# A linear attention and FFN kernel on one core: zero matmuls spread at the start, the last quarter stored in two parts, a new order of all steps

## The chip, the cores and the metric
The kernel runs on 1 core of one Trainium2 chip. The metric is device time in microseconds (us); the median of several executions is compared.

## The reference
Linear ("cosformer") attention on q, k, v of 8 batches x 8 heads x 576 positions x 64, followed by a feed-forward network (FFN) on the 4608 x 512 rows that it gives.

```python
r = np.maximum(x, 0.0)                            # phi, of q and of k
q_p, k_p = concat([r * c, r * s], axis=-1)        # c, s: cos and sin of pi/2 * pos / S
kv  = np.einsum('bhsf,bhsd->bhfd', k_p, v)
z   = np.sum(k_p, axis=2)
num = np.einsum('bhsf,bhfd->bhsd', q_p, kv)
den = np.einsum('bhsf,bhf->bhs', q_p, z)[..., None] + 1e-06
x   = (num / den).transpose(0, 2, 1, 3).reshape(4608, 512)
h   = x @ w_in                                    # w_in: 512 x 2048
out = np.maximum(0.01 * h, h) @ w_out             # w_out: 2048 x 512, out: 4608 x 512 float32
```

## The kernel before
The rows are worked in nine groups g: the first 512 positions of each of the 8 batches (g = 0 to 7), and the 8 x 64 rows left over (g = 8). Groups 0 and 1 take a plain first matrix product (`f0.*`, `f1.*`), and group 0 a plain second one (`F0.*`). All others use a form with seven products for eight blocks (Strassen-Winograd): DVE forms sums of blocks (X of x, S of the activations g, W and T of the weights), PE does the products, and DVE or ACT combine them.

Nothing schedules the kernel but one string, `ORDER` (L31 to L136). Each token is a step, `name[:engine][@slot]`; the program walks through the tokens in turn and emits the instructions of each step, so the order in the string is the order on every engine's queue. `:A`, `:D` and `:P` put a step on ACT, DVE or POOL, and `@` names the slot of a buffer or of a PSUM bank that its tile takes. What a step waits for follows from the tiles that it reads and overwrites. The steps that matter here:

- `i.n`: one matmul of zeros (L295), 128x128 by 128x512, into a PSUM slot of its own. 14 run in one slot before all else, and 16 more stand in the order between real work.
- `Lq`, `Lk`, `Lv`, `Lw1`, `Lw2`, `lq`, `lk`, `lv`: loads, all issued by SP. `cw`, `w`: casts of weights to f16. `v0.c`: cast of a quarter of v. `rq`, `rk`: relu of q or k. `kt`: k times the angles (DVE).
- `qt0.jp.hg`, `qo0.jp.hg`: the q turn of batch 0 on PE, a quarter each, and its copy to `qpT`. `kv0`, `ko0`: the kv sums and their copy. `n`, `N`: numerators on PE, and the division (DVE, three instructions: `den`, `rden`, `xs`). `xt`, `xo`: transpose of x and its copy; `xT`: the same by a DMA transpose, from group 2 on.
- `f`, then `e` (plain) or `b s u y z a c e d` (seven products): the first FFN product and what takes it out of PSUM. `F g.n.tt.h`: product n of the second one, half `tt` of the rows, half `h` of the depth, four matmuls each.
- `S g.n`: sums of activations. Product 1 starts a chain X in PSUM; `M g.1` copies it out (`mid`), and product 2 (`F g.2`) then adds on top of the same bank. `O g.n` adds a chain and a kept part to a quarter of the result in `osb`, and `D g.n` stores that quarter.

For g = 8 a quarter's rows belong to two halves of the partitions, so a store is a pair: SP stores one half, ACT the other. The quarters n = 3 and n = 5 are taken out and stored in two parts (`result_apart`, `store_apart`), n = 2 and n = 4 whole.

Of the kernel before, what the change touches and what calls it, by code (L numbers as in the profile page):

```python
# [11 lines left out]
ALU = mybir.AluOpType  # L12

P = 128
# [33 lines left out]
lq2@3 kv1.1@1 F0.2.14 ko1.1:A F0.0.14 n1.0.1@0 O0.2:D@3 N1.0.1 F0.3.12 F0.3.14 rq2.1:A F0.1.6 F0.1.8
rq2.0:P lk2@2 xt1.1.0@1 xt1.0.0@0 q2.3.0:P q2.0.1:P q2.2.0:P O0.3:D@0 q2.1.1:D lv2.0@1 n1.1.1 N1.1.1
O0.0:A@1 xt1.0.1@0 F0.1.10 xo1.0.1:D q2.3.1:A xo1.0.0:A xo1.1.0:A F0.1.12 f1.2.0@0 f1.0.0@1  # L50
xt1.1.1@0 lk3@0 lv2.1 f1.4.0 q2.0.0:D q2.1.0:P rk2.1:P rk2.0:A xo1.1.1:A f1.1.0 F0.1.14 kt2.0.0
kt2.1.0 kt2.0.1 T1 f1.3.0 f1.4.2 f1.2.2 f1.1.2 f1.0.2 f1.3.2 v2.1:P q2.2.1:D v2.0:A O0.1:A@2 e1.0
e1.1 kt2.1.1 T3 T2 T4 f1.5.0 qT2.0 lq3@3 f1.5.2 e1.2 f1.10@1 rk3.0:A f1.11 kv2 kt3.0.0 f1.6@0 e1.5
kt3.0.1 ko2:A rk3.1:A f1.7 e1.3 rq3.1:A n2.0 f1.12@1 N2.0 f1.13 e1.6 rq3.0:P q3.1.0:A q3.0.0:P n2.1
qT2.1 lv3.0@1 q3.2.0:A lv3.1 kt3.1.0 N2.1 q3.0.1:P f1.8@0 q3.3.0:P q3.1.1:P f1.9 S1.1a n2.2
F1.2.0.0@1 f1.14@1 f1.15 lq4@2 N2.2 n2.3 F1.1.0.0@0 F1.1.1.0 F1.2.1.0 q3.3.1:D e1.4 S1.1b S1.2a e1.7
F1.1.0.1 F1.1.1.1 F1.2.1.1 F1.2.0.1 v3.1:P v3.0:A M1.1:A F1.6.0.0@0 F1.6.1.0 N2.3 S1.1c S1.2b S1.3c
S1.2c F1.6.0.1 F1.6.1.1 kt3.1.1 S1.3a W0.3:D M1.6 W1.3:D S1.3b S1.4a kv3 xT2 F1.7.1.0 F1.7.0.0
F1.7.0.1 X2.1:D X2.2:D ko3:A q3.2.1:A f2.0.1 b2.0:A f2.1.1 f2.0.5 f2.0.6 u2.0:D X2.3:P s2.0:A f2.0.2
# [77 lines left out]
def kernel(  # L137
# [28 lines left out]
    NG = B + 1  # L166
# [950 lines left out]
```

## Time and profile before
| | us |
|---|---|
| median of 3 executions | 274.07 (274.07 to 275.02) |
| the profiled execution | 273.9 |
| its span | 271.9 |
| PE, DVE, ACT, POOL busy | 264.6, 210.1, 182.2, 79.7 |
| mean granted clock of PE | 1.00 |

PE, DVE, ACT, POOL and SP are TensorE, VectorE, ScalarE, GpSimd and SyncE; PEld is PE's loading of weights. A row of the timeline gives start, duration, engine, line, operation, `output<-input`, how many, and what ended the idle time before it. A row of windows gives, for each engine in order, busy us and instructions, and then the clock, the share of the 16 DMA engines and GB/s. A row of groups gives busy us and mean ns of one, then idle time ahead of it. The span is shorter than the execution's time by what the launch takes around it.

### The profile page before, as it was taken

To read this page: it belongs to the slowest core of one execution; us is meant where nothing else is said; L and a number is where in the kernel's file an instruction comes from. 1 tells how busy PE (TensorE), PEld (TensorE's weight loads), DVE (VectorE), ACT (ScalarE), POOL (GpSimd) and SP (SyncE) were. 2 spreads that over 40 slices of the span, in tenths; PEclk is the share of its full clock that TensorE was granted. 3 is DMA by queue.
4 is the path that set the end of the run, shared out by engine and by line. 5 is a ranking of instruction groups with operands and counts; after the bars stand their busy time and mean duration, and the time that the engine had idled before them with its cause. 6 is when DMAs were issued, how large, how long until landed. Compare 5 with 4: busy or idle time off the path is not lost.

```text
span 271.9 us, 7170 instructions
## 1 busy us (share of the span) xinstructions
PE 264.6 (97%) x2942; PEld 222.5 (82%) x2942; DVE 210.1 (77%) x419; ACT 182.2 (67%) x292; POOL 79.7 (29%) x86
## 2 busy tenths in 40 slices
PE   8989999999999999999999999999999999999993
PEld 2367555556899999999999999999999899999983
DVE  3653955898979999999889888798898668558652
ACT  4675895789558759887785786588765665554510
POOL 3321605654259310450263214083032004100000
PEclk9999999999999999999999999999999999999999
DMA  7999998999999599999997999572654361310225
GB/s 223 382 393 374 415 403 298 393 208 245 297 201 343 140 212 300 206 314 189 249 384 169 297 231 238 124 152 76 116 157 61 97 113 45 118 39 2 77 60 136
DMA packets 77264, 57.61 MB, mean 212 GB/s; under 512 B 49456, under 2 KB 65840, under 8 KB 76848
## 3 DMA queue, kind: packets, MB, share of 16 engines
q1 hardware_dynamic: 76624, 56.63, 76.0%
q10 hardware_dynamic: 608, 0.52, 0.6%
q8 instruction: 23, 0.38, 0.6%
q14 instruction: 9, 0.07, 0.1%
HBM read 36.70 MB, written 9.44 MB: 170 GB/s over the span
## 4 chain that ended last, share of the span: by engine, by line
PE 92%; DVE 3%; POOL 1%; ACT 1%; issue 0%; DVEq 0%
PE ps L846 35%; PE ps_f L763 32%; PE ps_h L624 8%; PE ps_o L647 5%; PE ps_idle L295 4%; PE ps_kv L444 3%; PE ps_num L544 3%; POOL vm L422 1%; PE ps_f L846 1%; PE ps_qt L520 1%; DVE kp L395 1%; DVE xs L560 1%; PE ps_qt L510 1%; PE ps_numh L579 0%; DVE T L677 0%
## 5 line engine op out<-in xcount | busy, mean ns | idle before, releaser
L846 PEld LDWEIGHTS <-g 128*128 128x128 f16 x640 | 62.2, 98 | 6.5
L787 ACT ACTIVATE g<-ps_f 128x512 f16<-128x512 f32 x84 | 48.5, 597 | 24.6 <-PE ps_f L763 13.8
L846 PE MATMUL ps<-w,g 128*128 128x256 f16 x496 | 64.9, 273 | 0.0
L763 PEld LDWEIGHTS <-w 128*128 128x128 f16 x448 | 48.3, 113 | 1.2 <-DVE u L422 0.2
L763 PE MATMUL ps_f<-xT,w 128*128 128x256 f16 x336 | 48.7, 273 | 0.0
L763 PEld LDWEIGHTS <-wext 128*128 128x128 f16 x336 | 36.2, 114 | 0.7 <-issue 0.2
L846 PE MATMUL ps<-T,ext 128*128 128x256 f16 x240 | 32.9, 273 | 0.0
L624 PE MATMUL ps_h<-xT,w 128*128 128x512 f16 (+1 forms) x144 | 29.4, 356 | 0.0
L846 PEld LDWEIGHTS <-ext 128*128 128x128 f16 x256 | 24.8, 98 | 2.5
L677 DVE TENSOR_TENSOR ps_f<-ps_f,u 128x512 f32<-128x512 f32 x28 | 19.5, 695 | 9.1 <-PE ps_f L763 6.9
L763 PE MATMUL ps_f<-X,wext 128*128 128x256 f16 x176 | 26.0, 273 | 0.0
L677 DVE TENSOR_TENSOR y<-ps_f,s 128x512 f32<-128x512 f32 x28 | 19.2, 686 | 7.5 <-PE ps_f L763 4.8
L624 PEld LDWEIGHTS <-w 128*128 128x128 f16 x144 | 15.7, 114 | 10.2
L420 ACT COPY u<-ps_f 128x512 f32<-128x512 f32 x22 | 12.9, 587 | 13.5 <-PE ps_f L763 13.4
L633 ACT ACTIVATE g<-ps_h 128x1024 f16<-128x1024 f32 x16 | 16.0, 1024 | 6.5 <-PE ps_h L624 6.4
L787 ACT ACTIVATE g<-y 128x512 f16<-128x512 f32 x28 | 17.7, 633 | 3.6 <-DVE y L677 3.6
L560 DVE TENSOR_TENSOR xs<-ps_num,rden 128x512 f16<-128x512 f32 x28 | 19.4, 691 | 1.0
L420 ACT COPY ps_f<-ps_f 128x512 f32<-128x512 f32 x28 | 16.1, 575 | 5.0 <-PE ps_f L763 4.3
L422 POOL CAST vm<-vst 128x1152 f16<-128x1152 f32 (+1 forms) x10 | 14.3, 1431 | 16.6 <-DMA vst<-in_v_dram 11.5
L677 DVE TENSOR_TENSOR osb<-ps,ext 128x512 f32<-128x512 f32 x23 | 15.7, 684 | 3.5 <-PE ps L846 3.2
L395 DVE TENSOR_TENSOR kp<-kst,ang 128x1152 f16<-128x1152 f16 x24 | 17.7, 766 | 0.2 <-ACT kst L385 0.2
L846 PE MATMUL ps<-ext,g 128*128 128x256 f16 x128 | 17.4, 273 | 0.0
(131 smaller groups left out, 433.3 us busy)
## 6 DMA issues: line engine op xcount, KB each, us to landing
out_dram<-osb SPq DMA_DIRECT2D x32, 256.0 KB, 3.6
qst<-in_q_dram SPq DMA_DIRECT2D x7, 1024.0 KB, 7.4
kst<-in_k_dram SPq DMA_DIRECT2D x6, 1152.0 KB, 8.2
vst<-in_v_dram SPq DMA_DIRECT2D x12, 576.0 KB, 6.0
w2st<-in_moe_w_out_dram SPq DMA_DIRECT2D x3, 1024.0 KB, 9.8
ext<-in_moe_w_in_dram SPq DMA_DIRECT2D x4, 512.0 KB, 9.5
kst<-in_k_dram SPq DMA_DIRECT2D x4, 288.0 KB, 5.7
vst<-in_v_dram SPq DMA_DIRECT2D x4, 288.0 KB, 7.1
```

Source lines behind the costliest of these rows:

```text
L295: nc.tensor.matmul(ps, lhsT=blank[:, 0:P], rhs=blank)
L395: nc.vector.tensor_tensor(out=st["kp", b][:, lo:hi, :, f * D : (f + 1) * D].rearrange("p c j (x y) -> p (c j) x y", y=2), in0=halved("k", ...
L420: nc.scalar.copy(o, i)
L422: eng.tensor_copy(o, i)
L560: nc.vector.tensor_tensor(out=xs, in0=ps[:, :, 0 : 4 * NE].rearrange("p a (b e) -> p a b e", e=NE)[:, :, :, 0:D], in1=rden.rearrange("p (a ...
L624: nc.tensor.matmul(ps[:, m % 2, lo:hi], lhsT=w1[m // 4, c][0][:, w1[m // 4, c][1], m % 4 : 512 : 4], rhs=xT[:, lo // P : hi // P, c, :], s ...
L633: nc.scalar.activation(g_tile(g)[:, 2 * i : 2 * i + 2, :], st["h", g, i], AF.Lrelu)
L647: nc.tensor.matmul(st["ps_o", g, tt], lhsT=st["g", g][:, m, tt * P : (tt + 1) * P], rhs=w2[:, m, :], start=(m == 0), stop=(m == NFT - 1),)
L677: eng.tensor_tensor(out=o, in0=a, in1=b, op=op)
L763: nc.tensor.matmul(ps[:, mi * HT : (mi + 1) * HT], lhsT=a[:, c, 2 * r0 + mi : 512 : 4], rhs=b[:, c], start=(n in (1, 5) and mi == 0 and c ...
L787: nc.scalar.activation(g_tile(g)[:, m : m + 2, r * HT : (r + 1) * HT], {"a": A, "c": y22, "e": E, "d": B_}[e].rearrange("p (m t) -> p m t" ...
L846: nc.tensor.matmul(ps[:, tt], lhsT=a[:, i, tt * P : (tt + 1) * P], rhs=b[:, i], start=(first and i == 0), stop=(i == NPR - 1 and (apart or ...
```

## The change
1. `ORDER` is another string throughout: the same steps in another sequence, with other engines for some of the copies and casts, and other slots. The 16 zero matmuls `i.n` stand at other places.
2. The quarter n = 4 of group 8 is taken out and stored in two parts too: `O8.4` and `D8.4` become `O8.4.0`, `O8.4.1`, `D8.4.0`, `D8.4.1`.

```diff
 ORDER = """
-Lk0.0@1 Lq0.0@2 i.14@0 rq0.0:P rk0.0:P qt0.0.0@1 qt0.1.0@0 i.12@0 qo0.0.0:A Lk0.2 kt0.0.0 kt0.0.1
-rk0.2:D i.3@1 i.5@1 i.2@1 Lq0.1 Lk0.1 qo0.1.0:A rq0.1:P rk0.1:A i.7@1 Lk0.3 Lv0.0@0 qt0.0.1 i.1@0
-i.15@0 i.10@0 i.11@0 rk0.3:D Lv0.1 qo0.0.1:A v0.0:A Lv0.3 Lv0.2 Lw1.0@3 Lw1.3 kt0.3.1 kt0.1.0
-kt0.1.1 v0.1:D i.9@0 i.0@0 i.13@0 qt0.1.1@1 i.4@0 kv0.0 qo0.1.1:A ko0.0:A kt0.3.0 v0.2:A kt0.2.1
...
+Lq0.0@1 Lk0.0@0 rk0.0:A Lk0.2 rk0.2:D kt0.0.0 kt0.2.1 kt0.2.0 kt0.0.1 Lq0.1 rq0.0:P Lk0.1 rk0.1:D
+kt0.1.0 kt0.1.1 i.0@0 qt0.0.0@0 Lk0.3 i.9@1 i.7@1 i.1@1 qt0.1.0@1 qo0.0.0:A i.5@1 i.14@0 i.11@1
+rq0.1:A Lv0.0@2 Lv0.1 Lv0.2 Lv0.3 Lw1.0@3 i.6@1 qt0.0.1 i.4@0 qo0.1.0:A qt0.1.1@1 i.2@0 Lw1.2 Lw1.1
+Lw1.3 rk0.3:A kt0.3.0 kt0.3.1 v0.2:D qo0.0.1:A i.3@0 v0.0:P v0.1:P kv0.0 qo0.1.1:A ko0.0:A n0.0.0@0
...
+lq8.2@0 rq8.2:A d5.3 F4.3.0.1 F5.1.1.0 b6.0:D X6.3:P X6.2:P f6.0.3 f6.0.2 f6.0.6 a6.0 u6.0:A
+F5.1.1.1 F5.1.0.1 D3.5 qT7.1 f6.1.1 f6.1.5 X6.4:P rq8.1:P S5.1c S5.2a N7.0 O4.3@2 f6.0.7 rq8.0:A
+S5.1b S5.3c M5.1:D S5.2b S5.2c y6.0 z6.0 q8.1.1:A q8.0.0:D F5.2.1.0 F5.2.1.1 F5.2.0.0 D4.3 lq8.3@1
...
 def result_apart(g, n, tt):
...
-        tt_op(osb, chain(g, n, tt)[0][:, tt], {5: t3, 3: t2}[n][:, part], ALU.add)
+        tt_op(osb, chain(g, n, tt)[0][:, tt], {5: t3, 3: t2, 4: t1}[n][:, part], ALU.add)
 def store_apart(g, n, tt):
-        store_tail(2 * (n == 5) + tt, 1, st["osb", g, n, tt])
+        store_tail(2 * (n != 3) + tt, int(n != 4), st["osb", g, n, tt])
...
-                    if g == NG - 1 and n in (3, 5):
+                    if g == NG - 1 and n in (3, 4, 5):
                         step(f"O{g}.{n}.{tt}", result_apart, g, n, tt)
                         step(f"D{g}.{n}.{tt}", store_apart, g, n, tt)
...
-                elif g < NG - 1 or n in (2, 4):
+                elif g < NG - 1 or n == 2:
                     step(f"O{g}.{n}", result, g, n)
                     step(f"D{g}.{n}", store, g, n)
```

At the start, ACT's queue from its first q copy to its second kv copy, before (a row is line, operation, output and input by name and number, shape; `qpT_224` and `qpT_239` are the two halves of the turned q, `r_147` holds relu of q and k, `vm_161` the cast v, `kv0_163` the kv sums):

```order
L420 CAST qpT_224<-ps_qt_188 128x2x512
L420 CAST qpT_239<-ps_qt_205 128x2x512
L385 ACTIVATE r_147<-kst_180 128x2x9x32
L420 CAST qpT_224<-ps_qt_248 128x2x512
L420 CAST vm_161<-vst_246 128x9x64
L420 CAST qpT_239<-ps_qt_292 128x2x512
L420 CAST kv0_163<-ps_kv_311 128x2x2x66
L420 CAST vm_161<-vst_246 128x9x64
L420 CAST kv0_163<-ps_kv_379 128x2x2x66
```

And after, where `qpT_241` and `qpT_278` are the two halves:

```order
L385 ACTIVATE r_147<-kst_182 128x2x9x32
L420 CAST qpT_241<-ps_qt_200 128x2x512
L385 ACTIVATE r_147<-qst_180 128x1024
L420 CAST qpT_278<-ps_qt_224 128x2x512
L385 ACTIVATE r_147<-kst_182 128x2x9x32
L420 CAST qpT_241<-ps_qt_259 128x2x512
L420 CAST qpT_278<-ps_qt_280 128x2x512
L420 CAST kv0_163<-ps_kv_311 128x2x2x66
L420 CAST kv0_163<-ps_kv_380 128x2x2x66
```

The two casts of v have left ACT, a second relu of k and one of q have come to it; the last of the four q copies stands directly ahead of the first kv copy in both.

DVE's queue around the copy M5.1, after (`y22` is the last product sum of group 5, `ps_f` the first FFN product in PSUM, `ext` holds sums and kept parts, `g_2801` the activations of group 5, `ps_7` the chains of the second product):

```order
L677 TENSOR_TENSOR y22_179<-ps_f3_1354,s5_178 128x512
L422 COPY ps_f2_1353<-ps_f0_1351 128x512
L677 TENSOR_TENSOR ext_96<-g_2801 128x2x256
L677 TENSOR_TENSOR ext_96<-ext_96,g_2801 128x1024
L555 TENSOR_SCALAR den_3197<-ps_num_3109 128x8
L559 RECIPROCAL rden_3199<-den_3197 128x8
L560 TENSOR_TENSOR xs_3196<-ps_num_3109,rden_3199 128x512
L677 TENSOR_TENSOR osb_3202<-ps_7_2872,ext_96 128x512
L677 TENSOR_TENSOR ext_96<-g_2801 128x2x256
L677 TENSOR_TENSOR g_2801<-g_2801 128x2x256
L422 COPY ext_96<-ps_7_3128 128x512
L677 TENSOR_TENSOR ext_96<-ext_96,g_2801 128x2x256 x2
```

Before, that copy is ACT's (`ps_7_3153`), here with its neighbours on ACT:

```order
L385 ACTIVATE qtl_3128<-qtl_3128 128x8x64
L420 COPY s5_178<-ps_f1_1353 128x512
L420 COPY u1_177<-ps_f2_1354 128x512
L787 ACTIVATE g_2749<-y22_179 128x2x256
L420 COPY ext_96<-ps_7_3153 128x512
L787 ACTIVATE g_3203<-ps_f0_1352 128x2x256
L787 ACTIVATE g_3203<-ps_f1_1353 128x2x256
L420 COPY ps_f1_1353<-ps_f3_1355 128x512
L408 ACTIVATE qp_3248<-qtl_3128,sin_t_142 128x8x64
```

The copy `ext_96<-ps_7` has moved from ACT, where it stood among copies out of the first FFN product, to DVE, where it stands behind a division (`den`, `rden`, `xs`), a result (`osb`) and four sums.

SP's queue at the end, before (each row one store; `64x256` is a part of a quarter, `64x2x256` a whole one):

```order
L904 DMA out_0_dram<-osb_4210 128x2x256
L895 DMA out_0_dram<-osb_4275 64x256
L909 DMA out_0_dram<-osb_4273 64x2x256
L895 DMA out_0_dram<-osb_4309 64x256
L895 DMA out_0_dram<-osb_4311 64x256
L909 DMA out_0_dram<-osb_4329 64x2x256
L895 DMA out_0_dram<-osb_4333 64x256
```

And after:

```order
L895 DMA out_0_dram<-osb_4278 64x256
L904 DMA out_0_dram<-osb_4169 128x2x256
L895 DMA out_0_dram<-osb_4307 64x256
L895 DMA out_0_dram<-osb_4311 64x256
L895 DMA out_0_dram<-osb_4280 64x256
L895 DMA out_0_dram<-osb_4325 64x256
L895 DMA out_0_dram<-osb_4337 64x256
```

Behind the last whole store of an earlier group stood two parts, a whole quarter and a part; now five parts stand there. ACT issues the other half of each in the same sequence.

More of the change, by code (lines that the diff above doesn't have):

```diff
@@ new lines @@
+Lw1.3 rk0.3:A kt0.3.0 kt0.3.1 v0.2:D qo0.0.1:A i.3@0 v0.0:P v0.1:P kv0.0 qo0.1.1:A ko0.0:A n0.0.0@0
+n0.1.0@1 N0.0.0 v0.3:P N0.1.0 kv0.1 i.12@0 i.15@0 xt0.0.0@0 ko0.1:A cw.0:A n0.0.1@0 i.13@1 i.10@1
+N0.0.1 Lw1.4 cw.2:P Lw1.5 Lw1.7 Lw1.8 Lw1.6 n0.1.1 N0.1.1 xo0.0.0:A xt0.1.0@0 cw.1:A f0.2.a@1
+xt0.0.1@1 xo0.0.1:D f0.0.a@0 xo0.1.0:A i.8@0 xt0.1.1@0 cw.3:D cw.4:D f0.1.a f0.1.c Lk1.0 f0.1.b
+Lq1@1 cw.8:D xo0.1.1:A rk1.0:P kt1.0.0 W0.1:D cw.5:A f0.1.d f0.0.b f0.3.a rq1.0:D rq1.1:D q1.1.1:D
+q1.0.1:D q1.0.0:D f0.0.c f0.0.d f0.0.e f0.1.e f0.3.c f0.2.c f0.2.d f0.2.e f0.3.d f0.3.e e0.1 f0.4.a
@@ new lines @@
+f0.5.a Lw2.0@0 kt1.0.1 w0.0:D q1.1.0:D q1.3.0:D Lw2.1@3 q1.2.1:P f0.5.d f0.6.a@1 q1.2.0:P f0.6.d
+f0.7.a f0.7.d f0.4.d cw.7:A Lk1.1 Lv1.0 e0.0 f0.12@0 f0.13 cw.6:A e0.3 f0.14@1 e0.2 e0.6 f0.15
+f0.8@0 e0.7 f0.9 f0.10@1 e0.4 f0.11 w0.2:A qt1.0@0 e0.5 F0.2.0 F0.3.0 F0.0.0@0 F0.0.2 F0.1.0@1
+qo1.0:A w1.0:D q1.3.1:D F0.1.2 qt1.3@0 F0.3.2 F0.1.4 qt1.1@1 w1.2:A rk1.1:A qo1.3:D kt1.1.0 v1.0:D
+W0.2:D qt1.2@0 F0.0.4 F0.3.4 F0.3.6 qo1.1:A Lw2.2@2 w2.0:D kv1.0@1 F0.2.2 F0.2.4 ko1.0:A F0.2.6
+F0.0.6 F0.3.8 w2.2:P Lw2.3.0 F0.2.8 n1.0.0@1 F0.3.10 Lw2.3.2 qo1.2:A n1.1.0@0 w3.0:A Lv1.1 lq2@3
@@ new lines @@
+a3.2 d3.1 kt5.0.1 z3.2 f3.3.1 F2.3.0.0 F2.3.0.1 y3.2 N4.3 e3.2 b3.3:A rk5.1:A f3.3.6 O2.3@2 f3.3.2
+f3.3.5 F2.4.1.0 f3.2.4 kt5.1.1 kt5.1.0 u3.3:A f3.3.7 c3.2 s3.3:A y3.3 a3.3 c3.3 d3.2 F2.4.1.1
+F2.4.0.1 f3.3.3 O2.4@0 z3.3 S3.1a f3.3.4 d3.3 xT4 kv5 qT5.0 rq6.0:P q5.3.1:D S3.2a F3.1.0.0@1
+F3.1.1.0 rq6.1:A e3.3 qT5.1 q6.1.0:P q6.2.0:P D2.5 F3.1.1.1 f4.0.1 b4.0:A F3.1.0.1 X4.1:D S3.1b
+f4.0.5 s4.0:A M3.1:A F3.6.0.0@0 f4.1.1 X4.2:D S3.3b S3.1c S3.2c ko5:D X4.3:D f4.0.6 F3.6.1.0 u4.0:D
+n5.0 f4.0.2 S3.3a a4.0 S3.2b X4.4:D f4.0.3 f4.0.7 F3.2.0.0 F3.2.1.0 z4.0 e4.0 b4.1:A F3.6.0.1
@@ L877, in result_apart @@
     def result_apart(g, n, tt):
-        osb = out_tile(g, HC)
+        osb = out_tile(0 if n == 4 else g, HC)
         st["osb", g, n, tt] = osb
         part = slice(tt * HC, (tt + 1) * HC)
-        tt_op(osb, chain(g, n, tt)[0][:, tt], {5: t3, 3: t2}[n][:, part], ALU.add)
+        tt_op(osb, chain(g, n, tt)[0][:, tt], {5: t3, 3: t2, 4: t1}[n][:, part], ALU.add)
     def store_apart(g, n, tt):
-        store_tail(2 * (n == 5) + tt, 1, st["osb", g, n, tt])
+        store_tail(2 * (n != 3) + tt, int(n != 4), st["osb", g, n, tt])
     def out_tile(g, n):
```

174 lines of the change are left out of this document (77 added, 97 removed).

## The prediction

> **What bounds the kernel now.** I read the page first (busy shares and the clock), then the busy times by window, then the chain and the timeline of the first 20 us and of the last 5, then the waits of the weight loads.
>
> ```profile
> span 271.9 us, 7170 instructions
> PE 264.6 (97%) x2942; PEld 222.5 (82%) x2942; DVE 210.1 (77%) x419; ACT 182.2 (67%) x292; POOL 79.7 (29%) x86
> ...
> PEclk9999999999999999999999999999999999999999
> ```
> ```profile
> 8.00:16.00 8.00, 7.03 (x103) 3.28 (x97) 4.48 (x12) 5.77 (x8) 1.95 (x3) 1.00 1.04 390
> ...
> 20.00:44.00 24.00, 24.00 (x193) 14.64 (x190) 15.05 (x26) 19.26 (x21) 7.18 (x6) 1.00 1.00 375
> 44.00:268.00 224.00, 223.42 (x2546) 199.34 (x2544) 184.25 (x357) 150.69 (x254) 66.28 (x64) 1.00 0.74 186
> ```
> PE is the bound: 24.00 of 24.00 us busy from 20 to 44, and 223.42 of 224.00 from 44 to 268, at full clock. All waits after 44 us are worth 0.6 us together. The matmuls are the same 2942 after the change, so time can come only from three places: the start (up to about 20 us), where PE spins on zero matmuls for want of data; those 0.6 us; and the tail behind the last matmul, which ends at about 267.7. What a new order can lose is not bounded in that way: a wait can appear at any step.
>
> The start, by the chain (start, duration) and by the timeline:
>
> ```profile
> 13.44 0.59 PE ps_qt L520 x16
> ...
> 14.05 1.01 ACT qpT L420
> 15.06 0.37 ACT kv L420
> ...
> 15.48 0.43 PE ps_numh L579 x8
> ...
> 16.37 0.69 DVE xs L560
> ...
> 17.40 0.69 DVE xs L560
> ```
> ```profile
> 1.19 5.93 PE L295 MATMUL ps_idle<-blank 128*128 128x512 f16 x15 [1.19 <-DVE blank L290]
> ...
> 7.72 1.93 ACT L420 CAST qpT<-ps_qt 128x1024 f16<-128x1024 f32 x2 [2.75 <-PE ps_qt L520]
> ...
> 9.54 0.70 ACT L385 ACTIVATE r<-kst 128x576 f16<-128x576 f32 x1
> ...
> 10.46 2.98 PE L295 MATMUL ps_idle<-blank 128*128 128x512 f16 x7
> ...
> 12.04 1.65 DVE L395 TENSOR_TENSOR kp<-r,ang 128x576 f16<-128x576 f16 x3
> 12.34 0.68 POOL L422 CAST vm<-vst 128x576 f16<-128x576 f32 x1 [2.63 <-DMA vst<-in_v_dram]
> ...
> 33.78 2.32 PE L647 MATMUL ps_o<-w,g 128*128 128x512 f16 x10
> ```
> Seven zero matmuls (10.46 to 13.44, 0.43 each, because each waits for the one before it in the same PSUM slot) stand in PE's queue ahead of the last quarter of the q turn, qt0.1.1. That quarter runs at 13.44, its ACT copy at 14.05, the copy of the first kv sums at 15.06, the first numerators at 15.48, and then one division each 1.03 us (16.37, 17.40). FFN1 of group 0 follows, and its FFN2 begins at 33.78.
>
> **The change part by part.** *Zero matmuls and the start.* The number stays (30). In the new order three stand ahead of qt0.1.0, four ahead of qt0.0.1, one ahead of qt0.1.1, two ahead of kv0.0. Walked by hand with the durations above: qt0.1.1 is done at about 11.7 rather than 14.03, and ACT becomes the chain. It runs the copy of qt0.0.0 from 7.7 (1.0), the relu of half of q (its 1024 columns taken as a copy's 1.0), the copy of qt0.1.0 (1.0), the relu of a quarter of k (0.70), the copy of qt0.0.1 (1.0, to 12.5, which frees the PSUM slot that kv0.0 needs), the copy of qt0.1.1 (to 13.5) and the first kv copy (0.37, to 13.9). The first numerators come at 13.9 rather than 15.48: a lead of 1.6. Two casts of v leave ACT and DVE for POOL; both fit ahead of kv0.0 at 0.68 each. The two early k products go to DVE earlier, which had idle time there (4.48 busy of 8.00).
>
> Does the lead last to 33.78? The rest of this stage is FFN1 with ACT freeing each slot of PSUM:
>
> ```profile
> L633 ACT ACTIVATE g<-ps_h 128x1024 f16<-128x1024 f32 x16 | 16.0, 1024 | 6.5 <-PE ps_h L624 6.4
> ```
> In the new order ACT has the weight casts cw.7 and cw.6 (about 1.0 each, as any 128x1024 pass) between the first of these activations, so that f0.14 and f0.8 wait some 0.5 for their slots, and the fourth division's transposes cost another 0.2 where PE has nothing else. I take FFN2's start at 32.9: a start term of -0.9. Its bounds: -1.4 (no such wait), and -0.3 if the casts on POOL take twice as long, which delays kv0.0 and all behind it by 0.6.
> The Trainium skill, page "GPSIMD Engine Reference", section "1. Specifications", speaks against moving the casts: it says that POOL and VectorE share SBUF interfaces and that POOL is held up by VectorE instructions with two SBUF inputs, as the k products are. The rows above do not bear that out: the POOL cast at 12.34 lies wholly beside k products (12.04 to 13.69) and took 0.68. By the rule the start term would be about -0.3, by the row -0.9.
>
> *The middle.* The whole order of some 1,400 steps is other. What can be gained is bounded by the 0.6 us above. For what can be lost I looked for places where an off-path step moved to a fuller engine. One stands out: M5.1, the copy of the X chain of group 5, moves from ACT to DVE and there stands behind, in turn, the sums S5.1c and S5.2a, the division N7.0, the result O4.3, and S5.1b and S5.3c, while PE's F5.2.1.0, which overwrites that chain, has no other PE step between. Prices, as start-to-start times on DVE, with the copy's own duration and PE's pace:
>
> ```profile
> 184.37 0.68 DVE L677 TENSOR_TENSOR y<-ps_f,s 128x512 f32<-128x512 f32 x1
> 184.97 0.16 DVE L555 TENSOR_SCALAR den<-ps_num 128x8 f32<-128x8 f32 x1
> ...
> 186.01 0.41 DVE L677 TENSOR_TENSOR ext<-g 128x512 f16<-128x512 f16 x1
> 186.34 0.68 DVE L677 TENSOR_TENSOR g<-g 128x1024 f16<-128x1024 f16 x1
> 186.94 0.34 DVE L414 TENSOR_SCALAR qp<-qtl,cos_t 128x512 f16<-128x512 f16 x1
> ...
> L422 DVE COPY s<-ps_f 128x512 f32<-128x512 f32 x6 | 4.1, 688 | 1.7 <-PE ps_f L763 1.2 <-issue 0.2
> ...
> 264.00 1.04 PE L846 MATMUL ps_f<-T,ext 128*128 128x256 f16 x8
> ...
> 264.88 1.04 PE L846 MATMUL ps_f<-w,g 128*128 128x256 f16 x8
> ```
> A 512-wide f32 step takes 0.60 (184.37 to 184.97), a division 1.04 (184.97 to 186.01), a sum of 512 f16 0.33, of 1024 f16 0.60. From the end of y5.3: b6.0 0.60, S5.1c 0.33, S5.2a 0.60, N7.0 1.04, O4.3 0.60, two sums 0.66, the copy 0.69, together 4.5, and some 0.2 for semaphores. PE does eleven steps of four matmuls from the same instant, 0.44 each (eight in 0.88, 264.00 to 264.88): 4.8. So it is nearly even, and a wait of 0 to 0.9 follows, the upper end if ACT's output of the third unit, which S5.1c reads, is one activation late; I take 0.2. Before, two of these eight copies were on DVE already (M2.1, M6.1), each with two PE steps between, and all waits together were 0.6, so that the move by itself need not cost.
> Other new waits are bounded by nothing below 0, and by about three such places (1.5) from above; I take 0.4. Old waits gone: 0.6 of 0.6 at most, taken as 0.6, since their places have all moved. Middle: 0.0 (-0.6 to +1.5).
>
> *The DMAs.* SP's loads keep their sequence for the most part. Between 8 and 16 us all 16 DMA engines are full (share 1.04), so the early loads can't come sooner: the lead eats the slack of what they feed. The transpose of group 2's x is the nearest:
>
> ```profile
> L500 SPq DMA_TRANSPOSE xT<-xs x1: 1902/1902/1902, 71.4 to 71.4; - x1
> L763 PE MATMUL ps_f<-xT,w x12: 272/272/273, 77.5 to 79.6; 128*128 128x256 f16 x12
> ...
> DMA to landing us min/median/max: 4.6/4.6/4.6
> ```
> Issued at 71.4, landed at 76.0, first read at 77.5: 1.5 of slack, more than the lead. Cost 0.
>
> *The tail.* O8.4, one sum of 512 and one pair of stores, becomes two sums of 256 and two pairs, so that SP and ACT issue 6 stores of 64x256 each at the end instead of 4, and one wide one instead of two.
>
> ```profile
> 267.75 0.42 DVE L677 TENSOR_TENSOR osb<-ps_f,ext 128x256 f32<-128x256 f32 x1 [0.24 <-PE ps_f L846]
> 268.26 0.56 SPq L895 DMA_DIRECT2D out_dram<-osb  x1
> 268.31 0.79 ACTq L895 DMA_DIRECT2D out_dram<-osb  x1
> ...
> L895 SPq DMA_DIRECT2D out_dram<-osb x2: 482/486/491, 265.5 to 266.4; - x2
> L895 ACTq DMA_DIRECT2D out_dram<-osb x2: 507/516/526, 265.5 to 266.4; - x2
> ...
> out_dram<-osb SPq DMA_DIRECT2D x3, 64.0 KB, 2.0
> out_dram<-osb ACTq DMA_DIRECT2D x3, 64.0 KB, 2.2
> ...
> out_dram<-osb SPq DMA_DIRECT2D x1, 64.0 KB, 2.4
> out_dram<-osb ACTq DMA_DIRECT2D x1, 64.0 KB, 2.6
> ```
> With E the end of the last matmul, the last store was issued at E+0.59 (268.26 against 267.67). Now each queue issues five stores of about 0.5 in the last stretch, D8.4.0, D8.4.1, D8.5.0, D8.3.1 and D8.3.0, from about E-1.15, so the fifth is issued at about E+1.05: 0.45 later. Against this its landing, slowed to 2.4 and 2.6 us by the wide store just ahead of it, should take the 2.0 and 2.2 of the lone ones: 0.4 sooner. The two leave +0.1 (-0.4 if the issues don't queue; +0.4 if the landing stays slow).
> By the Trainium skill, page "DMA: Bandwidth & Descriptors", section "Issuing engines are not separate DMA queues", issuing is usually cheap beside the transfer; the rows give 0.49 and 0.52 for each issue of these small stores. By that rule the tail would be -0.3.
>
> *Sum*, against the profiled execution's 273.9 (span 271.9 and 2.0 around it): -0.9 + 0.0 + 0.1 = -0.8, so 273.1. The median of the runs, 274.07, lies 0.17 above that execution; with it I forecast 273.3.
>
> **The rivals.**
> R1, faster: the start gives all its 1.4, the old waits of 0.6 vanish and nothing new comes. 274.07 - 1.4 - 0.6 + 0.1 = 272.2; say 272.0 to 272.7. For it: nothing after 44 us has to wait by the walk but M5.1. Against: a new order of all steps with no wait at all.
> R2, the lead is lost: group 0 starts sooner but PE then meets data that the full DMA engines bring no sooner (weights of w_out, group 2's transposes with 1.5 of slack), or the zero matmuls are merely replaced by waits, and the change doesn't do what it says. Time 274.1. Against: 1.5 is more than 0.9.
> R3, slower: the backlog on DVE ahead of a mid copy comes in most batches, not at M5.1 alone. At 0.5 for each of the 7 Strassen batches from 2 on it costs 3.5, so 273.3 - 0.2 + 3.5, less 0.4 of the new waits that it replaces, or 276.2; it decides the sign from three batches on (over 1.0) and passes 0.5% from five. Against: the other seven such copies are on ACT after the change, and DVE has 39.75 us idle from 44 to 268.
> R4, slower: the clock falls back in the start because the zero matmuls now stand in short groups with idle PE between. Price: the 15 first zero matmuls took 5.93, 0.40 each, where the FFN2 matmuls of the same width take 0.23 (ten in 2.32 at 33.78). If the first 15 matmuls' worth of work again ran at that pace, it would cost up to 2.4: 275.7. Before, PE was busy 7.03 of 8.00 between 8 and 16 us and the clock stood at 1.00.
> The Trainium skill, page "TensorE: Matmul & The Clock Gate", section "Part 1: The HAM clock gate (the "warmup" mystery)", says that the clock falls after an idle window of about 3.4 us; no gap in my walk is longer than 0.6.
>
> **How the numbers follow.** My forecast (272.7 to 274.0) 0.50; R1 0.25; R2 0.13; R3 0.08; R4 0.04. The range 272.0 to 274.8 takes in the forecast, R1 and R2 and the upper end of the middle term (+1.5); it leaves out R3 and R4. A measurement of this kernel tells about 0.5% (1.4 us) from no change: faster is below 272.7 (R1, and the lower edge of the forecast: 0.30), slower above 275.4 (R3 and R4: 0.12), and the same 0.58.
>
> **What would show it.** Start: the first numerators at about 13.9 and group 0's FFN2 at about 32.9. Middle: PE idle of about 0.6 from 44 us on, with 0.2 at F5.2.1.0. Tail: the last pair of stores issued at E+1.05, landed in 2.0 to 2.2. It would be wrong if PE shows idle stretches of over 0.5 ahead of the F steps of several batches (R3), a clock under 1.00 in the first windows (R4), or the same 33.8 for group 0's FFN2 (R2).

## The result and the profile after

The changed kernel takes 282.01 us (median of 4 runs, 280.67 to 283.09) where the kernel before took 274.44 (4 runs, 274.07 to 275.02): ratio 1.0272, 95% interval 1.0222 to 1.0322. The profiled execution is one of 283.09, at the slow end of the four. 273.3 (272.0 to 274.8) was forecast.

The page of the changed kernel, where the clock of PE dips in one place, two thirds through:

```profile
span 281.1 us, 7171 instructions
PE 267.6 (95%) x2942; PEld 223.2 (79%) x2942; DVE 217.1 (77%) x435; ACT 179.3 (64%) x284; POOL 70.8 (25%) x79
...
PEclk9999999999999999999999999959999999999999
```

Busy time by window, after (the columns are PE, PEld, DVE, ACT, POOL, then clock, share of the DMA engines, GB/s):

```profile
24.00:80.00 56.00, 53.52 (x565) 32.56 (x564) 44.36 (x80) 40.79 (x50) 16.18 (x16) 1.00 0.99 306
80.00:140.00 60.00, 59.83 (x727) 56.23 (x726) 54.13 (x111) 43.56 (x77) 24.17 (x24) 1.00 1.07 258
140.00:176.00 36.00, 36.00 (x456) 33.73 (x455) 32.96 (x64) 28.68 (x48) 12.82 (x12) 1.00 0.81 198
176.00:184.00 8.00, 3.89 (x67) 3.40 (x60) 2.25 (x5) 2.00 (x4) 0.00 (x0) 0.91 1.07 188
184.00:190.00 6.00, 6.00 (x39) 4.44 (x38) 4.80 (x10) 3.03 (x5) 3.75 (x4) 0.55 0.87 175
190.00:260.00 70.00, 70.00 (x705) 65.40 (x703) 54.53 (x107) 41.69 (x75) 8.44 (x9) 1.00 0.35 73
```

And three of these windows before, the first, the fourth and the fifth:

```profile
24.00:80.00 56.00, 55.80 (x590) 35.47 (x588) 42.92 (x79) 42.37 (x52) 24.02 (x20) 1.00 1.04 314
...
176.00:184.00 8.00, 8.00 (x83) 7.71 (x82) 6.40 (x12) 7.03 (x13) 6.61 (x8) 1.00 0.71 152
184.00:190.00 6.00, 6.00 (x68) 5.69 (x67) 4.90 (x12) 5.04 (x9) 1.92 (x3) 1.00 0.24 65
```

The 9.2 us by which the span grew lie in the main in three places. From 24 to 80 us PE idles 2.48 us rather than 0.20. From 176 to 184 it idles 4.11 rather than 0. And from 184 to 190 it is busy all the time but at a clock of 0.55: 39 matmuls instead of 68, some 2.7 us lost (6.00 x 0.45). The rest nearly cancels: PE idles 0.59 us less ahead of 24, 0.13 more from 80 to 140 and 0.27 more at the tail. From 190 to 260 it is full at a clock of 1.00 in both.

What PE waits for at 179 is seen in the timeline: the division that completes the input of xT6, the k product kt7.1.0, SP's queue, and f6.0.1, the first reader.

```profile
171.10 0.69 DVE L560 TENSOR_TENSOR xs<-ps_num,rden 128x512 f16<-128x512 f32 x1
...
173.19 0.75 DVE L395 TENSOR_TENSOR kp<-kst,ang 128x1152 f16<-128x1152 f16 x1
```
```profile
174.09 1.29 SPq L251 DMA_DIRECT2D qtl<-in_q_dram  x2
175.54 2.83 SPq L488 DMA_TRANSPOSE qpT<-qp  x1
178.41 3.49 SPq L500 DMA_TRANSPOSE xT<-xs  x1
```
```profile
183.48 1.04 PE L763 MATMUL ps_f<-xT,w 128*128 128x256 f16 x4 [4.11 <-DMA xT<-xs]
```
And the issue of xT6 before:
```profile
171.43 1.76 SPq L500 DMA_TRANSPOSE xT<-xs  x1
```
The input of xT6 is complete at 171.8. But in SP's queue `lq8.1@3 qT7.0` stand ahead of `xT6`. lq8.1 needs stage slot 3, in which the k of batch 7 lies until kt7.1.0, in this order its last reader, is done (173.94); the expectation of e1 below calls it kt7.1.1, which stands earlier here and is the last reader in the kernel before. Then lq8.1 holds SP for 1.3 us and qT7.0 for 2.8, so that xT6 is issued at 178.41, 6.6 us after it could have been, and PE reads its result at 183.48. Before, xT6 was issued at 171.43, with lq8.1 behind it.

The first numerators came about when the walk had them: 13.57 (13.9 forecast, 15.48 before). But group 0's FFN2 did not come sooner:

```profile
13.57 0.67 PE L579 MATMUL ps_numh<-kv,qpT 128*128 128x66 f16 x16 [0.47 <-ACT kv L420]
```
```profile
33.33 0.68 DVE L422 CAST w<-w2st 128x1024 f16<-128x1024 f32 x1
```
```profile
34.06 2.32 PE L647 MATMUL ps_o<-w,g 128*128 128x512 f16 x10 [0.64 <-DVE w L422]
```
It begins at 34.06 (33.78 before), held by the cast w0.0, which DVE reached at 33.33 behind q and k work of batch 1.

The tail after, SP's and ACT's stores of the last 8 us:

```profile
275.33 3.05 SPq L895 DMA_DIRECT2D out_dram<-osb  x5
...
276.62 0.42 DVE L677 TENSOR_TENSOR osb<-ps_f,ext 128x256 f32<-128x256 f32 x1 [0.39 <-PE ps_f L846]
```
```profile
L895 SPq DMA_DIRECT2D out_dram<-osb x6: 482/547/595, 273.1 to 277.8; - x6
L895 ACTq DMA_DIRECT2D out_dram<-osb x6: 496/557/818, 273.1 to 278.1; - x6
```
The last matmul ends at 276.59 and the last pair is issued at 277.8 and 278.1, that is 1.2 to 1.5 after it rather than 0.6. SP issues the five from 275.33 one behind the other. From the last matmul to the span's end it is 4.5 us rather than 4.24: +0.27, where +0.1 (-0.4 to +0.4) was forecast.

### The profile page after: what moved, and what is told of

It reads as the page before. It is cut to its first block, busy times and chain, and to the rows that moved or that the text cites. A ratio compares the mean times of both kernels' runs of the same rounds, so it can differ in the third digit from the quotient of the medians.

```text
span 281.1 us, 7171 instructions
## 1 busy us (share of the span) xinstructions
PE 267.6 (95%) x2942; PEld 223.2 (79%) x2942; DVE 217.1 (77%) x435; ACT 179.3 (64%) x284; POOL 70.8 (25%) x79
## 4 chain that ended last, share of the span: by engine, by line
PE 80%; DVE 8%; DMA 7%; SPq 1%; ACT 1%; issue 1%; DVEq 0%
PE ps L846 31%; PE ps_f L763 30%; PE ps_o L647 4%; DMA xT<-xs 4%; PE ps_h L624 4%; PE ps_idle L295 3%; DMA qst<-in_q_dram 3%; PE ps_num L544 3%; PE ps_kv L444 3%; DVE xs L560 1%; DVE kp L395 1%; PE ps_f L846 1%; SPq L488 1%; PE ps_qt L520 1%; DVE w L422 1%
## 5 line engine op out<-in xcount | busy, mean ns | idle before, releaser
L787 ACT ACTIVATE g<-ps_f 128x512 f16<-128x512 f32 x84 | 49.1, 597 | 36.6 <-DVE ps_f L677 18.9
L846 PE MATMUL ps<-w,g 128*128 128x256 f16 x496 | 66.1, 277 | 0.0
L763 PE MATMUL ps_f<-xT,w 128*128 128x256 f16 x336 | 49.3, 274 | 4.5 <-DMA xT<-xs 4.5
L763 PEld LDWEIGHTS <-wext 128*128 128x128 f16 x336 | 36.8, 114 | 0.7
L677 DVE TENSOR_TENSOR osb<-ps,ext 128x512 f32<-128x512 f32 (+1 forms) x24 | 15.7, 663 | 6.4 <-PE ps L846 6.1
L560 DVE TENSOR_TENSOR xs<-ps_num,rden 128x512 f16<-128x512 f32 x28 | 19.4, 691 | 1.0
L395 DVE TENSOR_TENSOR kp<-kst,ang 128x1152 f16<-128x1152 f16 x24 | 19.1, 838 | 1.0 <-ACT kst L385 0.7
L420 ACT COPY ps_f<-ps_f 128x512 f32<-128x512 f32 x25 | 14.3, 573 | 6.3 <-PE ps_f L763 5.8
L422 POOL CAST vm<-vst 128x1152 f16<-128x1152 f32 (+1 forms) x9 | 9.5, 1056 | 34.7 <-DMA vst<-in_v_dram 24.1
```

The lines of the kernel that those rows point to most:

```text
L395: nc.vector.tensor_tensor(out=st["kp", b][:, lo:hi, :, f * D : (f + 1) * D].rearrange("p c j (x y) -> p (c j) x y", y=2), in0=halved("k", ...
L420: nc.scalar.copy(o, i)
L422: eng.tensor_copy(o, i)
L560: nc.vector.tensor_tensor(out=xs, in0=ps[:, :, 0 : 4 * NE].rearrange("p a (b e) -> p a b e", e=NE)[:, :, :, 0:D], in1=rden.rearrange("p (a ...
L677: eng.tensor_tensor(out=o, in0=a, in1=b, op=op)
L763: nc.tensor.matmul(ps[:, mi * HT : (mi + 1) * HT], lhsT=a[:, c, 2 * r0 + mi : 512 : 4], rhs=b[:, c], start=(n in (1, 5) and mi == 0 and c ...
```

## The experiments

**One load moved behind xT6 (e1).**
```diff
-S5.1a lq8.1@3 qT7.0 e5.2 xT6 b5.3:A ...
+S5.1a qT7.0 e5.2 xT6 lq8.1@3 b5.3:A ...
```


> The changed kernel with one load, lq8.1, moved behind the transpose xT6 in SP's queue, and nothing else. Theory A (SP's queue: xT6 stands behind lq8.1, which waits until 173.94 for its stage slot, whose last reader is the k product kt7.1.1, and behind qT7.0; xT6 was issued at 178.41 although its input was ready at 171.8, and the long idle of PE then let the clock fall): qT7.0 goes at about 172.2, xT6 at about 175.1, lands at about 180.0, PE waits 0.5 to 1.2 us at f6.0.1 instead of 4.3, and as the wait is short the granted clock stays at 1.00; about 276, that is 5.5 to 6.5 faster than the changed kernel. Rival B (the transpose is slow for the load on the DMA engines, or DVE's backlog is what delays PE there): xT6 lands about as late, or PE waits for DVE instead; 280 to 282.

Measured: 275.89 us, ratio 1.0052 (1.0024 to 1.0079). SP's queue, PE's row of f6.0.1 (eight matmuls, with the step ahead of it and no idle time before it), and the window after:

```profile
168.55 3.00 SPq L488 DMA_TRANSPOSE qpT<-qp  x1
172.45 1.78 SPq L500 DMA_TRANSPOSE xT<-xs  x1
174.60 1.52 SPq L251 DMA_DIRECT2D qtl<-in_q_dram  x2
```
```profile
179.40 1.04 PE L763 MATMUL ps_f<-xT,w 128*128 128x256 f16 x8
```
```profile
180.00:184.00 4.00, 4.00 (x44) 3.80 (x43) 3.86 (x9) 2.71 (x5) 2.50 (x3) 1.00 1.14 207
```
xT6 goes at 172.45, PE does not wait for it, and the clock stays at 1.00. One token is worth 2.2% (1.0272 against 1.0052), some 6 us. qT7.0 had been ready long before, at 168.55: it too stood behind the waiting load, so that the wait which was expected to remain (0.5 to 1.2) is 0.

**xT6 ahead of both (e1b).**
```diff
+S5.1a e5.2 xT6 qT7.0 lq8.1@3 b5.3:A ...
```


> The changed kernel with xT6 ahead of both qT7.0 and lq8.1 in SP's queue. Theory A: xT6 is issued at about 171.9 and lands at about 177, before PE needs it at 179.1, so the wait at f6.0.1 is 0; qT7.0 is issued some 3.5 us later than it could, at 175.4, and lands at 180 to 181, so that n7.0, the step behind f6.0.1, waits 0.5 to 1.5 instead. Clock 1.00. About 275.5 to 276.5, like the kernel with lq8.1 alone moved. Rival B: 280 to 282.

Measured: 276.49 us, ratio 1.0042 (1.0015 to 1.0068), the same as e1. PE waits 0.7 us at n7.0, one step behind f6.0.1, as expected.

**PE kept busy while it waits (e2).**
```diff
+    def hold():
+        for _ in range(18):
+            nc.tensor.matmul(banks(6, 0)[0], lhsT=w2[:, 0, 0:P], rhs=w2[:, 0, :], skip_group_check=True)
...
-... a5.3 f6.0.1 ko7:D n7.0 ...
+... a5.3 hold f6.0.1 ko7:D n7.0 ...
```


> The changed kernel with 18 matmuls of no use (128x128 by 128x512, into the PSUM bank that f6.0.1 then overwrites) right ahead of f6.0.1, 3.9 us at 0.216 each, so that PE is busy while xT6 is on its way. Theory A with the clock as a second part: the wait of 4.3 at f6.0.1 stays, filled by these matmuls, but the clock stays at 1.00 after it, and the 2.5 us that PE lost from 183.5 to 189.4 by running at half clock are gone: about 279.5. Rival C (the slow stretch after 183.5 has nothing to do with the idle time ahead of it): the windows from 184 to 190 still show a clock of 0.50 to 0.66, and the time stays at 282.

Measured: 280.79 us, ratio 1.0200 (1.0160 to 1.0240). PE's timeline, the windows, one of its waits, and a sum on DVE ahead of that:

```profile
179.10 4.05 PE L979 MATMUL ps_f<-w 128*128 128x512 f16 x18
183.15 0.60 PE L763 MATMUL ps_f<-xT,w 128*128 128x256 f16 x4
```
```profile
184.00:186.00 2.00, 2.00 (x20) 1.86 (x19) 1.92 (x4) 1.76 (x4) 1.97 (x2) 1.00 1.11 270
186.00:188.00 2.00, 2.00 (x21) 1.92 (x20) 1.97 (x4) 1.51 (x3) 1.95 (x2) 1.00 1.19 170
```
```profile
PE ps L846 <- DVE ext L422: 0.7, 1, 0.7
```
```profile
186.18 1.65 DVE L677 TENSOR_TENSOR ext<-ext,g 128x1024 f16<-128x1024 f16 x1
```
xT6 is as late as before, f6.0.1 runs at 183.15, and the clock stays at 1.00: the slow stretch came from the idle time ahead of it. Holding it brings 0.7% (1.0272 to 1.0200, 2.0 us; the intervals of the two overlap a little, so this is rough) of the expected 2.5. Part of the rest is the wait of 0.7 us: PE reaches F5.2.1.0 before M5.1 is done on DVE. That is not a matter of full pace alone, since e1 runs at full pace and has no wait there. In e2 a sum ahead of M5.1, S5.2a, took 1.65 us beside a sum on POOL, where it took 0.68 in e1.

**The same fault put into the kernel before (e3).**
```diff
-... O4.4@2 xT6 n7.0 ... lq8.1@1 lq8.2@2 ...        (qT7.0 earlier)
+... O4.4@2 lq8.2@2 qT7.0 xT6 n7.0 ... lq8.1@1 ...
```


> The kernel before, with lq8.2 and qT7.0 moved to stand ahead of xT6 in SP's queue, lq8.2's stage slot having as last reader the k product kt7.1.1, as in the changed kernel; nothing else. Theory A: lq8.2 waits until kt7.1.1 ends at 172.7, takes 1.4, qT7.0 2.9, so that xT6 is issued at about 177 instead of 171.43 and lands at about 182 instead of 175.75; f6.0.1, which ran at 176.25, waits 5 to 6 us, and PE's clock falls to half for several us after it: 274.1 + 5.5 + 2.5 = 282. Rival B (the delay belongs to something else in the changed order): under 276.

Measured: 279.18 us, ratio 1.0154 (1.0110 to 1.0199). SP's queue, PE's two waits and the window:

```profile
173.82 1.29 SPq L251 DMA_DIRECT2D qtl<-in_q_dram  x2
175.27 3.11 SPq L488 DMA_TRANSPOSE qpT<-qp  x1
178.43 1.82 SPq L500 DMA_TRANSPOSE xT<-xs  x1
```
```profile
180.40 0.43 PE L544 MATMUL ps_num<-kv,qpT 128*128 128x66 f16 x8 [1.65 <-DMA qpT<-qp]
...
182.85 0.63 PE L763 MATMUL ps_f<-xT,w 128*128 128x256 f16 x4 [1.16 <-ACT g L787]
```
```profile
180.00:184.00 4.00, 2.36 (x24) 1.87 (x25) 0.23 (x2) 1.51 (x3) 1.12 (x1) 1.00 0.97 217
```
The queue issues xT6 at the same time (178.43 against 178.41), and the kernel before gets 4.2 us slower by it. It missed the expected 282: here n7.0 stands ahead of f6.0.1 on PE, so the idle time falls into pieces of 1.65 and 1.16 us with work between, and the clock stays at 1.00. Without the slow stretch the fault costs about 4; that the wait comes in one piece of 4.1 cost the changed kernel 2 to 2.7 more. The other executions agree: the mean clock is 0.988 to 0.994 in all four of the changed kernel, and 0.996 or more in all of e1, e2 and e3.

**The start alone (s1)**: the changed order up to F0.2.0, then the remaining tokens in the order of before.


> The changed order for the start alone (all steps up to group 0's second FFN product, with the zero matmuls apart), then the rest in the order of the kernel before, tail included. In the changed kernel the first numerators came at 13.57 instead of 15.48, but group 0's FFN2 began at 34.06 instead of 33.78, since its weights landed at 32.1 (31.2 before) and were cast by DVE only at 33.33. Theory A (the lead of the start is lost before 34 us): the first numerators at 13.6, FFN2 at 33.5 to 34.2, time as before, 273.8 to 275. Rival B (the start does give 0.9, and it is the later steps that lose it): FFN2 at 32.9, time 0.9 below the kernel before.

Measured: 275.73 us, ratio 1.0023 (1.0002 to 1.0044).

```profile
33.88 2.32 PE L647 MATMUL ps_o<-w,g 128*128 128x512 f16 x10
```
FFN2 comes at 33.88, as in the kernel before: the lead is gone by then, as theory A has it. The rest of theory A fits less well. The first numerators come at 14.43 rather than 13.6, the median lies above its 275, and PE idles 2.13 us from 24 to 80 (0.20 before), most of it soon behind the joint of the two orders: 0.98 at 44.35 for a cast of v on ACT, 0.49 at 42.35 for a weight cast on ACT. So the run shows that no lead arrives, and not what the start alone is worth.

**Four zero matmuls less in the kernel before (z1)**: `i.9`, `i.0`, `i.13` and `i.10` left out.


> The kernel before with four of the seven zero matmuls ahead of qt0.1.1 left out (12 in place of 16 in the order). Theory A (what the zero matmuls take is hidden in the start: FFN2 of group 0 needs weights that land at 31.2 and are cast by 32 to 33): qt0.1.1 runs at 11.8 instead of 13.44, the first numerators at 14 to 14.5 instead of 15.48, FFN2 at 32.3 to 33.0 instead of 33.78 at best; 273 to 274.2. Rival B (a lead at the numerators goes through to the end): 1.0 to 1.6 less, under 273.1. Rival C (fewer zero matmuls let the clock fall at the start): a clock under 1.00 in the windows up to 24 us, and over 275.

Measured: 274.35 us, ratio 0.9979 (0.9958 to 1.0001). The first numerators come at 14.36 rather than 15.48, FFN2 at 33.73 rather than 33.78. The interval just takes in 1. ACT shows where the lead ends, at the landing of a weight, for which the kernel before did not have to wait (the same cast ran at 18.45 there):

```profile
18.51 1.05 ACT L420 CAST w<-w1st 128x1024 f16<-128x1024 f32 x1 [1.07 <-DMA w1st<-in_moe_w_in_dram]
```

**The split alone (t1)**: O8.4 and D8.4 of the kernel before in two parts, at their old place.


> The kernel before with O8.4 and D8.4 in two parts each, at the place where they stood whole; nothing else. In the changed kernel the stretch from the end of the last matmul to the span's end was 4.5 us, before 4.24. Theory A (five stores of 0.5 to 0.55 queue on SP and ACT): the last pair is issued 0.4 to 0.6 later after the last matmul than before, it lands 0.2 to 0.5 faster, and the stretch is 4.2 to 4.6; time within 0.4 of the kernel before. Rival B (narrow stores land sooner and gain): 3.8 to 4.0.

Measured: 274.25 us, ratio 0.9976 (0.9953 to 0.9999). The last matmul ends at 267.12 and the span at 271.2: 4.1 us, between the theories' ranges and 0.15 less than before. What made the changed kernel's tail 4.5 is then not the split by itself. In t1 the last pair is issued at 267.9 and 268.2, 0.8 and 1.1 after the last matmul, 0.4 sooner than in the changed kernel, and the two stretches differ by 0.4. The changed order has `D8.4.1 D8.5.0`, so that a store whose sums are done by 273.6 stands among the five that SP issues from 275.33; in t1 `D8.5.0 D8.3.1` stand ahead of `D8.4.0`. No run moves that store, so that it is the cause is not shown.

**The early waits (f1, f2).** f1 moves five steps in e1:
```diff
 (moved:) Lq1 ahead of Lk1.0; rk1.0 and kt1.0.0 to kt1.0.1; n1.1.1 behind F0.1.10;
          T2 behind N1.1.1; S1.2a behind N2.2
```


> The changed kernel with lq8.1 behind xT6, and the four early waits that its trace shows taken away one by one in the order: the load of q of batch 1 ahead of that of k, with kt1.0.0 behind the q products (waits at 32.2 and 33.1: 0.2 and 0.8); n1.1.1 one FFN2 step later (50.1: 0.48); the weight sum T2, 1.5 us on DVE, behind xo1.0.0 and N1.1.1 (52.6: 0.51); the sum S1.2a behind the division N2.2 (70.3 and 78.3: 0.73 and 0.52). Theory A (each wait is DVE's or SP's order at that one place, 3.2 together): 1.5 to 3.2 less than with lq8.1 moved alone, 272.7 to 274.4, at or under the kernel before. Rival B (DVE is so full up to 90 us that a wait mended here turns up at the next place): 275 to 276.

Measured: 278.25 us, ratio 1.0117 (1.0079 to 1.0156). In f1 the weight sum W0.1 overwrites the staged k of batch 1 ahead of its relu, so that batch's sums are made from other data; the time is that of the same work. It is slower than e1, against both theories. The waits at n1.1.1 and S1.2a went, but FFN2 waited 1.31 us and began at 35.87, because DVE came to w0.0 at 35.13 rather than 33.33: W0.1 had waited for the landing of k until 29.24, two relus of q took 2.24 rather than 1.30, and kt1.0.0 now stood ahead of w0.0 too. This explains only a part. The profiled execution (276.97, mean clock 0.996) is 0.4 above e1's, while five of the eight have a mean clock of 0.987 to 0.991 and take 278 or more; what slows those is not in the profile and stays open. f2 keeps the last three moves and puts w0.0 ahead of kt1.0.1 instead.


> The changed kernel with lq8.1 behind xT6, and with four small moves against its early waits: the cast w0.0 ahead of kt1.0.1 on DVE (F0.2.0 waited 0.80 for it), n1.1.1 one FFN2 step later (0.48), T2 behind xo1.0.0 and N1.1.1 (0.51), S1.2a behind N2.2 (0.73). The loads of batch 1 stay where they are, since in the kernel f1 the cast w0.0 was held up by the later load of k. Theory A (each wait belongs to one place in DVE's order): 1.5 to 2.5 less than with lq8.1 moved alone, a ratio to the kernel before of 0.996 to 1.000. Rival B (DVE is so full that the waits turn up elsewhere): 1.004 to 1.006.

Measured: 274.69 us, ratio 0.9987 (0.9968 to 1.0007), 0.65% under e1. From 24 us on, its profile shows PE waiting for one thing only, in two places:

```profile
PE ps_f L763 <- DMA xT<-xs: 1.6, 2, 1.0
```
Moving four tokens took 1.8 us off (1.0052 to 0.9987): the waits of 24 to 80 us came from the order at single places and did not turn up again behind them. The four were moved together, so what each is worth is not shown.

**The later part by itself (s4e, s5).** s4e is the order of before up to f2.0.1, and then e1's.


> The order of the kernel before up to group 2's first FFN product (f2.0.1, at 77.5 us), then the rest in the changed order, lq8.1 behind xT6, tail in two parts. Theory A (apart from xT6 all that the changed order loses is lost ahead of 80 us): like the kernel before, ratio 0.997 to 1.002. Rival B (the rest of the changed order loses by itself, at M5.1 or at xT4): 1.004 or more.

Measured: 276.85 us, ratio 1.0072 (1.0047 to 1.0098): theory A fell. The trace has one large wait, at 124.7 us (PE), and what led to it on DVE and SP:

```profile
PE ps_f L763 <- DVE y L677: 1.9, 1, 1.9
```
```profile
123.93 0.69 DVE L677 TENSOR_TENSOR osb<-ps,ext 128x512 f32<-128x512 f32 x1 [2.94 <-DMA out_dram<-osb]
```
```profile
109.95 1.08 SPq L234 DMA_DIRECT2D qst<-in_q_dram  x1
111.07 4.55 SPq L662 DMA_DIRECT2D out_dram<-osb  x1
```
D0.1, a store left over from group 0, stands on SP behind two loads of v and one of q, is issued at 111.07 to 115.6 and lands at 123.8. The result that wants its slot holds DVE for 2.9 us, and `y` behind it holds PE. s5 moves that store ahead of the three loads:
```diff
-... D0.3 a3.1 lv5.0@1 ... lv5.1 v5.1:P lq6@2 D0.1 ...
+... D0.3 D0.1 a3.1 lv5.0@1 ... lv5.1 v5.1:P lq6@2 ...
```


> The kernel s4e (the order of before up to 77.5 us, then the changed order with lq8.1 behind xT6) with the store D0.1 moved ahead of lv5.0, lv5.1 and lq6 in SP's queue. Theory A (the old store lands late because it queues behind 2.3 MB of loads, and DVE's result waits for its slot): DVE's wait of 2.9 us for that landing is gone, PE's wait of 2.0 at 124.5 with it, the ratio falls from 1.007 to 0.998 to 1.001. Rival B (the store is as late wherever it stands, since the DMA engines are full; or DVE's own queue delays y): over 1.004.

Measured: 274.89 us, ratio 1.0005 (0.9986 to 1.0025): theory A. DVE's wait for the landing is gone. The same move in f2:


> The changed kernel with lq8.1 behind xT6, the four early mends of f2, and D0.1 moved ahead of lv5.0, lv5.1 and lq6. f2's trace showed one wait of 1.15 at 126.5 behind the same store. Theory A: 1.0 less than f2, a ratio of 0.994 to 0.997. Rival B: as f2, 0.998 to 1.001.

Measured: 274.75 us, ratio 0.9997 (0.9980 to 1.0013), a miss. Of f2's wait at 126.5 I had the wrong cause: it stays (the longest of the row below, 1.0 us) and PE waits there for xT4, not for the store.

```profile
PE ps_f L763 <- DMA xT<-xs: 1.4, 2, 1.0
```

**Both small edits together (g1)**: the kernel before with z1's and t1's edits.


> The kernel before with four of the seven zero matmuls ahead of qt0.1.1 left out and O8.4 in two parts: the two single parts together, each of which stood at a ratio of 0.998. Theory A (they add up): 0.995 to 0.997. Rival B (both were noise about 1): 0.999 to 1.001.

Measured: 273.62 us, ratio 0.9963 (0.9941 to 0.9985). The two parts add up to 0.4%, as theory A has it. FFN2 stands at 32.88 in its profile, but the first numerators stand at 13.43 there and at 14.36 in z1, with the same start, so that this is no gain of the edits: from the first numerators to FFN2 it is 19.4 us in both.

## Why the prediction was wrong

- **The start** was sized about rightly to 14 us and wrongly from there to 34 (-0.9 forecast, +0.28 measured at FFN2). The walk costed PSUM slots and ACT, and left out that w0.0 waits on DVE behind q and k work of batch 1, and that the weights land when the full DMA engines bring them. This is the rival R2, which had a chance of 0.13. A start shifts from one profile to the next (the order of before has its first numerators at 14.94 in t1, 15.48 in its own profile and 16.49 in e3), so the stretch from there to FFN2 says more: 18.3 us in these three, 20.5 in the changed kernel (19.9 to 20.5 in e1, e1b and e2), and 19.3 in f2 and f3, where w0.0 stands ahead of kt1.0.1. So w0.0's place took about half of the 2.2 that were lost. The other half is not traced; z1 and g1, with 19.4, lose 1.1, in z1 at the landing of a weight.
- **The DMAs** is the step that failed: "SP's loads keep their sequence for the most part", "Cost 0". In its place stands a wait of 4.1 us for xT6, with the slow stretch behind it; one load moved (e1) takes away some 6 of the 7.6 us by which the median grew. I looked at the one transpose whose slack the profile showed nearest the start (xT2, 1.5 us; in the changed kernel PE waits 0.36 even for it, at 79.05) and not at what stands ahead of each transpose in SP's new order, nor at which reader frees the slot of each load ahead of it. The order's text shows it: `lq8.1@3 qT7.0 e5.2 xT6` in place of `qT7.0 xT6 ... lq8.1@1`. Its price, 4.1 us of wait, is more than the whole range of 2.8. A store moved the same way (D0.1) costs another 2 us where the early part is that of before.
- **R4** had the right mechanism at the wrong place, with a chance of 0.04. The clock did fall, not between the zero matmuls but after 4.1 us of idle PE at 179 to 183, for 2.7 us of loss in the profile and 2.0 by e2. Two idle pieces of 1.65 and 1.16 us (e3) left it at 1.00, and so did the filled gap of e2. The rule that the prediction quotes from the Trainium skill, page "TensorE: Matmul & The Clock Gate", section "Part 1: The HAM clock gate (the "warmup" mystery)", agrees with all three; what was wrong was the sentence that no gap is longer than 0.6.
- **R3**, DVE's backlog, happened too, but from 32 to 79 us and not at the mid copies: 2.48 us of idle PE rather than 0.20, in six places, four of them behind DVE (1.8 together), one behind ACT (0.31) and one behind xT2 (0.36). f2's four moves took 1.8 off. "Other new waits" were bounded by 1.5 for "three such places".
- **M5.1** stayed within its bounds, 0 to 0.9: no wait in the changed kernel, where PE was slow just then, none at full pace in e1, f2, f3 and s4e, and 0.7 in e2, where xT6 came late and a sum ahead of the copy took 1.65 us.
- **The tail** (+0.1 forecast, +0.27 measured) is within its bounds. The fifth pair is issued late, 1.2 to 1.5 after the last matmul where the walk had 1.05; t1 shows that the split itself does not cost.
- **The casts on POOL** do cost something, on the other engine. The prediction judged the rule by the time of POOL's cast alone, 0.68 us. The rows below show the k products of the start, before and after (the three numbers are the least, the median and the greatest ns of one), and ACT's first kv copy after. A k product takes 0.45 us, and 0.91 to 0.92 where it runs beside a cast on POOL (the one at 12.4 before, the one at 11.6 after; another, at 11.0 after, takes 0.63). In the changed kernel the kv sums start only as the last of them ends (12.35 and 12.46; in s1, with the same start, the profile names that product as what they wait for), and ACT, which the walk had as the chain, idles 0.36 for them. So the sentence that the rows "do not bear that out" was wrong. The first numerators came early all the same; what casts on ACT and DVE would have given with this order was not tried.

```profile
L395 DVE TENSOR_TENSOR kp<-r,ang x8: 444/452/917, 7.6 to 13.3; 128x576 f16<-128x576 f16 x8
```
```profile
L395 DVE TENSOR_TENSOR kp<-r,ang x8: 451/454/910, 6.9 to 11.6; 128x576 f16<-128x576 f16 x8
```
```profile
13.14 0.38 ACT L420 CAST kv<-ps_kv 128x264 f16<-128x264 f32 x1 [0.36 <-PE ps_kv L444]
```

## What to carry to other kernels

When an order is searched anew, walk each in-order queue that issues DMAs as carefully as the engine that is the bound. For every transfer on the critical path write down what stands ahead of it on that queue, which reader frees the buffer of each of those, and how long each holds the queue. A wait in one piece on a full PE can cost half as much again if the clock falls behind it, as it did after 4.1 us here and not after 1.65, so price it with the slow stretch behind it, and try whether independent work can be put into it.

## What the runs showed of the hardware that was not expected

- A DMA transpose holds SP from 1.8 us (172.45 in e1) to 3.5 us (178.41 in the changed kernel), and a store issued behind loads held it 4.55 us (s4e), while stores of the tail take 0.55. A queue of a few such issues is several microseconds long without any wait in it.
- After 4.1 us without work PE ran at 0.55 of its clock from 184 to 190 us; 18 useless matmuls in that gap kept it at 1.00.
- VectorE was slowed by work on POOL beside it: a k product took 0.91 us beside a cast on POOL and 0.45 without (before and after), a sum of 128x1024 took 1.65 beside a sum on POOL (e2, 186.18) and 0.68 without (e1). POOL's own casts took 0.66 to 0.75.
